# Attention and two expert layers on one core: an order from latest times, values in column tiles, and unsplit scores for the first 8 pairs

## The chip, the cores and the metric

The kernel runs on one core of a Trainium2 chip. The metric is device time in microseconds, median of three runs; less is better. Engines in the tables: PE is TensorE (matmuls; PEld its weight loads), DVE is VectorE, ACT is ScalarE, POOL is GpSimd, SP is SyncE, which issues the transfers.

## What is computed

Attention with a threshold below the row's maximum, then two feed-forward layers, all in float32. The sizes are 4 batches, 8 heads, 576 positions, head size 64, width 512, inner width 2048:

```python
scores = 0.125 * q @ k.T
thresh = max(scores) - tau
scores = where(scores >= thresh, scores, -1e9) - max(scores)
attn = exp(scores) / (sum(exp(scores)) + 1e-9)
x = (attn @ v)                  # to tokens x 512
x = softplus(x @ w1_in) @ w1_out
out = relu(x @ w2_in) ** 2 @ w2_out
```

## The kernel before

**Pairs and groups.** Attention is done in 32 pairs of two heads; a pair has one batch, half of its 576 queries (288) and two heads. Four pairs make a group of 288 tokens; there are 8 groups. A pair goes through four steps. `a_prep` (lines 269 to 274) splits the loaded q and k into a rounded part in float32r (ACT casts, L271, L272) and a rest (a subtraction on POOL, for the first pair on DVE, L273, L274). `a_scores` computes scores in nine slices of 128 keys by 288 queries from three float32r products each (high by high, low by high, high by low): the two heads sit on partitions 0 to 63 and 64 to 127, so L290 works on two row tiles of the array; the last slice has the last 64 keys of both heads and is a product over all 128 rows (L295). ACT copies each slice out of PSUM to the buffer st (L298). `a_max` finds the maximum of each query on DVE (L305, L307, L310) with four ACT copies between (L309), and spreads it over partitions as mb, for the first four pairs with L313 and L314, later with two transfers. `a_soft` subtracts it and masks (DVE, L328, L331) and exponentiates (ACT, L332). `a_out` multiplies by the values in full-precision float32, ten products a pair (L344, L345), each with 128 stationary columns: 64 of values and 64 of ones, so that one half of a PSUM bank receives the result and the other half the denominator, in 64 equal rows. ACT copies both halves out (L346, L347), DVE makes the reciprocal from a transposing reduction (L349 to L351) and multiplies (L352).

**The layers.** Layer 1 runs on one group of 288 tokens after another: `m1_up` (L368 to L370, three float32r products for each slice), softplus (ACT, L378 to L380; DVE, L381), a split (L386, L387) and `m1_down` (L399 to L401). Layer 2 runs afterwards on 512 tokens at a time (L368 to L370 and L508 to L510). Weights arrive as 64-bit words and are converted by ACT and DVE (L241 to L244) and split by POOL (L255), some through PE (L249, L250).

**What sets the order.** Each step is recorded in a `Plan` (lines 42 to 147) with its engine, an estimated duration and a key. `emit` is a list scheduler: whichever engine is free first takes the ready step with the smallest key. The keys are written by hand: pair u's steps have keys about 2u, and block k of layer 1 (a 256-wide slice of the inner width) has key k + `LAG`, with `LAG` = 13. Each engine then executes its steps in the order found.

**Buffers that the change touches.** k_r, q_r (one each), v_t (two of 1024 columns), m and rb (two each), d.

Of the kernel before, what the change touches and what calls it, by code (L numbers as in the profile page):

```python
# [26 lines left out]
LAG = 13  # L27
SPREAD = 4
EARLY = 6
PREPDVE = 1  # L30
# [11 lines left out]
class Plan:  # L42
# [6 lines left out]
    SYNC, AFTER_PE, DRAIN, LOOK, DMA_START, DMA_END, BYTES_PER_NS = 200, 300, 130, {}, 1600, 950, 300  # L49
# [20 lines left out]
    def emit(self):  # L70

        first = len(self.done)
        n = len(self.ops)
        waits = [0] * (n - first)
        users = [[] for _ in range(n - first)]
        ready_at = [0] * (n - first)
        self.done += [None] * (n - first)
        for i in range(first, n):
            for d in self.ops[i][3]:
                if d < first:  # L80
                    ready_at[i - first] = max(ready_at[i - first], self.seen(d, self.ops[i][0]))
                else:
                    waits[i - first] += 1
                    users[d - first].append(i)
        future, ready, events = {}, {}, []
        engines = {op[0] for op in self.ops[first:]}
        for e in engines:
            future[e], ready[e] = [], []
            self.free.setdefault(e, 0)
            heapq.heappush(events, (self.free[e], e))  # L90

        def release(i):
            e, key = self.ops[i][0], self.ops[i][4]
            heapq.heappush(future[e], (ready_at[i - first], key, i))
# [5 lines left out]
        left = n - first  # L100
        while left:
# [13 lines left out]
            soon = [f for f in future[e] if f[0] <= t + self.LOOK.get(e, 0) and f[1] < LAG and (not ready[e] or f[1:] < ready[e][0])]  # L115
            if soon:
                f = min(soon, key=lambda f: f[1:])
                future[e].remove(f)
                heapq.heapify(future[e])
                t, i = f[0], f[2]  # L120
            else:
                _, i = heapq.heappop(ready[e])
# [4 lines left out]
            self.free[e] = t + ns  # L127
            end = t + ns
# [4 lines left out]
            order.append((t, len(order), fn))  # L133
            left -= 1
# [5 lines left out]
        for _, _, fn in sorted(order, key=lambda x: x[:2]):  # L140
            fn()
# [9 lines left out]
def kernel(ctx: ExitStack, tc: tile.TileContext, qT, kT, vp, tau, w1i, w1o, w2i, w2o, out):  # L151
# [45 lines left out]
    v_t = many(2, [128, 1024], "v_t")  # L197
    k_r, q_r = ap.tile([128, KW], F32, name="k_r"), ap.tile([128, HALF], F32, name="q_r")
# [3 lines left out]
    m_t, r_t, mr_t = many(2, [128, 11, 9], "m"), many(1, [32, 12, 9], "r"), many(2, [32, 2, 32], "mr")  # L202
    mb_t = many(2, [128, 2, HALF], "mb")
    rb_t, d_t = many(2, [128, HALF], "rb"), many(2, [128, 9], "d")
# [4 lines left out]
    w_t = ap.tile([128, 18], F32, name="w_t")  # L209
    m_d = [dram.tile([18, 32], F32, name=f"m_d{i}") for i in range(4)]  # L210
# [47 lines left out]
    def a_load(u, key):  # L258
        g, hp = divmod(u, HP)
        b, half = divmod(g, 2)  # L260
        P.add("SP", 600, lambda: SP.dma_start(k_r, kT[b, hp]), [], ["k_r"], key, 327680)
        P.add("SP", 600, lambda: SP.dma_start(q_r, qT[b, half, hp]), [], ["q_r"], key, 147456)

    def v_load(u, key):

        g, hp = divmod(u, HP)
        P.add("SP", 600, lambda: SP.dma_start(v_t[u % 2], vp[g // 2, hp]), [], [("v", u % 2)], key, 1 << 19)

    def a_prep(u, key):
        eng, E1, n1, n2 = ("DVE", DVE, 740, 370) if u < PREPDVE else ("POOL", POOL, 1520, 750)  # L270
        P.add("ACT", 330, lambda: ACT.copy(q_h, q_r), ["q_r"], ["q_h"], key)  # L271
        P.add("ACT", 630, lambda: ACT.copy(k_h, k_r), ["k_r"], ["k_h"], key)  # L272
        P.add(eng, n2, lambda: E1.tensor_tensor(q_l, q_r, f32(q_h), op=ALU.subtract), ["q_r", "q_h"], ["q_l"], key, lock=True)  # L273
        P.add(eng, n1, lambda: E1.tensor_tensor(k_l, k_r, f32(k_h), op=ALU.subtract), ["k_r", "k_h"], ["k_l"], key, lock=True)  # L274

    def a_scores(u, key):
# [5 lines left out]
        QK = ["k_h", "k_l", "q_h", "q_l"]  # L282
        for c in range(5):
            banks = [(y_ps[i], ("y", i)) for i in (2 * (c % 2), 2 * (c % 2) + 1)] if u < EARLY else [(a_ps[i], ("a", i)) for i in range(2)]
            cs = slice(128 * c, 128 * c + 128)
            if c < 4:
                def mms(banks=banks, cs=cs):
                    for n, (k, q) in enumerate(ops):
                        for o in range(2):
                            PE.matmul(banks[o][0][:, :HALF], k[half[o], cs], q[half[o]], start=(n == 0), stop=(n == 2))  # L290
                P.add("PE", 590 * cold, mms, QK, [b[1] for b in banks], key + 0.1 * c)
            else:
                def mms(bank=banks[0][0], cs=cs):
                    for n, (k, q) in enumerate(ops):
                        PE.matmul(bank[:, :HALF], k[:, cs], q, start=(n == 0), stop=(n == 2))  # L295
                P.add("PE", 400, mms, QK, [banks[0][1]], key + 0.1 * c)
# [3 lines left out]
    def a_max(u, key):  # L300
        i = u % 2
        st, ST = st_t[u % 3], [("st", u % 3, o) for o in range(2)]
        m, r, mr, md = m_t[i], r_t[0], mr_t[i], m_d[u % 4]
        M, R, MR, MD = ("m", i), "r", ("mr", i), ("md", u % 4)
# [29 lines left out]
    def a_out(u, key):  # L334
# [4 lines left out]
        rb, RB = rb_t[u % 2], ("rb", u % 2)  # L339
        half = [slice(0, 64), slice(64, 128)]  # L340
        for o in range(2):
            bank, BK = a_ps[o][:, :HALF], ("a", o)
            for c in range(4):
                P.add("PE", 486 * cold, lambda c=c, o=o, bank=bank: PE.matmul(bank, vt[:, 192 * c + 64 * o:192 * c + 64 * o + 128], e[:, 5 * o + c], start=(c == 0), stop=False), [E[o], V], [BK], key + o)  # L344
# [258 lines left out]
```

## Time and profile before

| | |
|---|---|
| median of three runs | 1166.75 us (1165.86 to 1168.1) |
| the profiled execution | 1168.44 us, span 1166.7 us |
| mean granted PE clock | 0.978 of full speed |
| busy: PE, DVE, ACT, POOL | 1117.3, 678.0, 685.9, 247.8 us |

The profiled execution lies 1.7 us above the median. Attention and layer 1 share the first 730 us or so, layer 2 takes the rest. A busy PE means that records of matmuls cover the time; a record is longer than its slot in the stream, so durations of PE are read below from start to start. A full-precision float32 product leaves two weight loads and two matmul records, a float32r product one of each.

### The profile page before, as it was taken

The numbers are of one execution on the slowest core, as the hardware profiler recorded it, in microseconds if no ns is written. First come the engines' busy times: TensorE is split into PE (matmuls) and PEld (weight loads), VectorE is DVE, ScalarE is ACT, GpSimd is POOL, SyncE is SP. The second block draws the span as 40 slices with busy tenths as digits, with TensorE's granted clock in tenths as the row PEclk, the third lists the DMA queues.
The fourth block names the chain that finished last, engine by engine and source line by source line (L and its number), as shares of the span: only waits on it lengthen the run. The fifth ranks groups of instructions, "written<-read, shape, count | busy, mean of one in ns | idle before, by whom it ended". The sixth has DMA issues, their size and how long they took to land.

```text
span 1166.7 us, 16963 instructions
## 1 busy us (share of the span) xinstructions
PE 1117.3 (96%) x6424; PEld 953.1 (82%) x6424; DVE 678.0 (58%) x962; ACT 685.9 (59%) x1560; POOL 247.8 (21%) x222
## 2 busy tenths in 40 slices
PE   4777899999999999999999999999999999999998
PEld 3554788898898888988988899988888888888887
DVE  5998988775765756757657645888332322322232
ACT  5888888777777677777776757865222222222222
POOL 3232532342222223222223121544000000000000
PEclk9787999999999999999999999999999999999999
DMA  5346442221221312212211104764010010000010
GB/s 181 103 137 208 163 153 71 80 68 56 84 61 56 100 46 62 94 51 71 79 56 64 49 12 159 237 188 144 27 47 1 4 51 1 1 37 1 1 37 19
DMA packets 39285, 89.10 MB, mean 76 GB/s; under 512 B 6180, under 2 KB 14884, under 8 KB 39204
## 3 DMA queue, kind: packets, MB, share of 16 engines
q1 hardware_dynamic: 39204, 88.03, 23.4%
q8 instruction: 50, 0.82, 0.3%
q14 instruction: 31, 0.25, 0.1%
HBM read 78.51 MB, written 9.50 MB: 75 GB/s over the span
## 4 chain that ended last, share of the span: by engine, by line
PE 86%; DVE 8%; ACT 2%; issue 2%; DMA 2%; POOL 0%; SPq 0%; DVEq 0%; POOLq 0%; ACTq 0%
PE h_ps L368 12%; PE h_ps L370 11%; PE h_ps L369 11%; PE a_ps L344 9%; PE y_ps L399 6%; PE y_ps L508 6%; PE y_ps L509 6%; PE y_ps L510 6%; PE y_ps L401 5%; PE y_ps L400 5%; PE a_ps L290 4%; DVE st L328 2%; PE a_ps L345 2%; DVE st L331 2%; DVE wraw L242 1%
## 5 line engine op out<-in xcount | busy, mean ns | idle before, releaser
L368 PE MATMUL h_ps<-x_h,wih 128*128 128x288 f32 x512 | 161.5, 315 | 7.3 <-DVE gt L381 5.7
L399 PE MATMUL y_ps<-g_h,woh 128*128 128x288 f32 x512 | 159.4, 311 | 0.0
L387 POOL TENSOR_TENSOR g_l<-gt,g_h 128x288 fp32r<-128x288 f32 x96 | 83.2, 872 | 340.8 <-ACT g_h L386 255.6
L370 PE MATMUL h_ps<-x_h,wil 128*128 128x288 f32 x512 | 153.2, 299 | 0.0
L369 PE MATMUL h_ps<-x_l,wih 128*128 128x288 f32 x512 | 151.4, 296 | 0.0
L401 PE MATMUL y_ps<-g_l,woh 128*128 128x288 f32 x512 | 151.1, 295 | 0.0
L344 PE MATMUL a_ps<-st,v_t 128*128 128x288 f32 x512 | 144.0, 426 | 7.4 <-ACT st L332 7.4
L400 PE MATMUL y_ps<-g_h,wol 128*128 128x288 f32 x512 | 150.9, 295 | 0.0
L488 ACT ACTIVATE r<-h_ps 128x512 f32<-128x512 f32 (+1 forms) x80 | 44.4, 555 | 151.5 <-PE h_ps L370 151.5
L489 DVE SCALAR_TENSOR_TENSOR r<-h_ps,r 128x512 f32<-128x512 f32 (+1 forms) x80 | 51.0, 638 | 135.9 <-ACT r L488 135.9
L381 DVE SCALAR_TENSOR_TENSOR gt<-h_ps,a_t 128x288 f32<-128x288 f32 x128 | 57.4, 451 | 124.2 <-ACT a_t L380 123.7
L344 PEld LDWEIGHTS a_ps<-st,v_t 128*128 128x128 f32 x512 | 99.5, 199 | 34.8 <-ACT st L332 9.1
L328 DVE TENSOR_TENSOR st<-st,mb 64x288 f32<-64x288 f32 (+1 forms) x128 | 124.5, 992 | 2.0 <-DMA mb<-m_d 0.9
L495 ACT CAST g_h<-r 128x512 fp32r<-128x512 f32 (+1 forms) x80 | 46.2, 578 | 125.9 <-PE y_ps L509 125.7
L369 PE MATMUL h_ps<-y_l,wih 128*128 128x512 f32 (+1 forms) x320 | 120.0, 375 | 0.0
L368 PE MATMUL h_ps<-y_h,wih 128*128 128x512 f32 (+1 forms) x320 | 119.2, 372 | 0.0
L370 PE MATMUL h_ps<-y_h,wil 128*128 128x512 f32 (+1 forms) x320 | 118.7, 371 | 0.0
L496 DVE TENSOR_TENSOR g_l<-r,g_h 128x512 fp32r<-128x512 f32 (+1 forms) x80 | 51.0, 637 | 110.8 <-ACT g_h L495 110.7
L509 PE MATMUL y_ps<-wol,g_h 128*128 128x512 f32 x288 | 114.1, 396 | 0.0
L508 PE MATMUL y_ps<-woh,g_h 128*128 128x512 f32 x288 | 114.1, 396 | 0.0
L510 PE MATMUL y_ps<-woh,g_l 128*128 128x512 f32 x288 | 114.0, 396 | 0.0
L368 PEld LDWEIGHTS h_ps<-x_h,wih 128*128 128x128 f32 x512 | 97.8, 191 | 18.7 <-DVE gt L381 7.8
(101 smaller groups left out, 2456.2 us busy)
## 6 DMA issues: line engine op xcount, KB each, us to landing
v_t<-in_vp SPq DMA_DIRECT2D x32, 512.0 KB
k_r<-in_kT SPq DMA_DIRECT2D x32, 320.0 KB
wraw<-in_w1i SPq DMA_DIRECT2D x16, 512.0 KB
wraw<-in_w1o SPq DMA_DIRECT2D x16, 512.0 KB
wraw<-in_w2i SPq DMA_DIRECT2D x16, 512.0 KB
wraw<-in_w2o SPq DMA_DIRECT2D x16, 512.0 KB
mb<-m_d SPq DMA_DIRECT2D x28, 288.0 KB
q_r<-in_qT SPq DMA_DIRECT2D x32, 144.0 KB
```

Source lines behind the costliest of these rows:

```text
L328: DVE.tensor_tensor(st[p0:p1, a:a + n], st[p0:p1, a:a + n], mb[p0:p1, o:o + 1].to_broadcast([p1 - p0, n, HALF]), op=ALU.subtract),
L344: P.add("PE", 486 * cold, lambda c=c, o=o, bank=bank: PE.matmul(bank, vt[:, 192 * c + 64 * o:192 * c + 64 * o + 128], e[:, 5 * o + c], sta ...
L368: PE.matmul(bank, wih[p][:, c, f], xh[c], start=(c == 0), stop=False)
L369: PE.matmul(bank, wih[p][:, c, f], xl[c], start=False, stop=False)
L370: PE.matmul(bank, wil[p][:, c, f], xh[c], start=False, stop=(c == 3))
L387: P.add(eng, ns, lambda j=j: e.tensor_tensor(g_hl[1][j], gt_t[j], f32(g_hl[0][j]), op=ALU.subtract), [("gt", j), ("g_h", j)], [("g_l", j)] ...
L399: PE.matmul(o, woh[p][:, j, es], g_h[j], start=first, stop=False)
L400: PE.matmul(o, wol[p][:, j, es], g_h[j], start=False, stop=False)
L401: PE.matmul(o, woh[p][:, j, es], g_l[j], start=False, stop=last)
L508: PE.matmul(o, g_h[j][:, ts], woh[p][:, j], start=first, stop=False)
L509: PE.matmul(o, g_h[j][:, ts], wol[p][:, j], start=False, stop=False)
L510: PE.matmul(o, g_l[j][:, ts], woh[p][:, j], start=False, stop=last)
```

## The change

1. **Order.** `emit` runs the list scheduler 24 times. After each round a backward pass works out, from the end of that round's order, how late each step could run, and these latest times are the keys of the next round; the shortest round by the plan's own estimates is used. `LAG` becomes 12 (the first round's keys), and some estimated durations change.
2. **Values in column tiles.** A pair's values are 8 products with 64 stationary columns, the two heads in the two halves of one PSUM bank, and one product of 128 columns for the last keys. The denominators are 8 products with 32 columns of ones, in four column tiles of another bank, and one of 128 columns. Each head's denominator arrives in two partial sums, so ACT copies four pieces across partitions (L441 of the changed kernel) and DVE adds them (L442). One eviction of 128 partitions takes the place of two of 64. The values' transfer shrinks from 512 to 320 KB.
3. **Scores without a split.** For the first 8 pairs (`RAW`) `a_prep` does nothing, and each slice of scores is one full-precision product of the loaded k and q in place of three float32r products. k_r and q_r have two buffers each; m and rb have one in place of two.

```diff
-LAG = 13
+LAG = 12
-PREPDVE = 1
+RAW = 8
...
+    def emit(self, rounds=24):
...
+        keys = [op[4] for op in self.ops[first:]]
+        best = None
+        for r in range(rounds):
+            self.free, self.bus, self.lock = dict(state[0]), *state[1:]
+            order = self.forward(first, users, keys)
+            length = max(self.free.values())
+            if best is None or length < best[0]:
+                best = length, order, self.done[first:], (self.free, self.bus, self.lock)
+            keys = self.backward(first, users, order)
...
     def a_prep(u, key):
...
+        if u < RAW:
+            return
...
+        if u < RAW:
+            ops, QK, last, ns = [(k_rt[u % 2], q_rt[u % 2])], [("k_r", u % 2), ("q_r", u % 2)], 0, [590, 590]
...
+        X, D = a_ps[0][:, :HALF], a_ps[1][:, :HALF]
+        AX0, AD = ("a", 0), ("a", 1)
+        for c in range(4):
+            def mms(c=c):
+                for o in range(2):
+                    PE.matmul(X[64 * o:64 * o + 64], vt[:, 256 * o + 64 * c:256 * o + 64 * c + 64], e[:, 5 * o + c], start=(c == 0), stop=False)
+            P.add("PE", (490 + 100 * (c == 0)) * cold, mms, E + [V], [AX0], key)
+        for c in range(0, 4, 2):
+            def mms(c=c):
+                for o in range(2):
+                    for i in range(2):
+                        a = 64 * o + 32 * i
+                        PE.matmul(D[a:a + 32], one_t, e[:, 5 * o + c + i], start=(c == 0), stop=False)
+            P.add("PE", (490 + 100 * (c == 0)) * cold, mms, E, [AD], key)
+        P.add("PE", 590 * cold, lambda: PE.matmul(X, vt[:, 512:], e[:, 4], start=False, stop=True), [E[0], V], [AX0], key)
+        P.add("PE", 490 * cold, lambda: PE.matmul(D, onb_t, e[:, 4], start=False, stop=True), [E[0]], [AD], key)
+        P.add("ACT", 310, lambda: ACT.copy(xf, X), [AX0], [XF], key - 0.5)
+        P.add("ACT", 310, lambda: ACT.copy(rb, D), [AD], [RB], key - 0.5)
...
+        for a in range(4):
+            b = a ^ 1
+            P.add("ACT", 220, lambda a=a, b=b: ACT.copy(d[32 * a:32 * a + 32, 1], d[32 * b:32 * b + 32, 0]), [DN], [("d2", u % 2)], key + 0.5)
+        P.add("DVE", 140, lambda: DVE.scalar_tensor_tensor(out=d[:, 0], in0=d[:, 0], scalar=1e-9, in1=d[:, 1], op0=ALU.add, op1=ALU.add), [("d2", u % 2)], [DN], key + 1)
```

**PE, one pair's products with the values in the middle of the program.** Before, the ten products of a pair stand together (a_ps are the two PSUM banks, st the exponentials, v_t the values):

```order
L295 MATMUL a_ps_145<-q_h,k_h 128x288
L295 MATMUL a_ps_145<-q_h,k_l 128x288
L295 MATMUL a_ps_145<-q_l,k_h 128x288
L344 MATMUL a_ps_146<-st_156,v_t_148 128x288 x2
L344 MATMUL a_ps_145<-st_156,v_t_148 128x288 x4
L345 MATMUL a_ps_145<-st_156,v_t_148 128x288
L344 MATMUL a_ps_146<-st_156,v_t_148 128x288 x2
L345 MATMUL a_ps_146<-st_156,v_t_148 128x288
L399 MATMUL y_ps_63<-g_h_132,woh_86 128x288
```

Now (L423 values in two column tiles, L430 denominators in four, L432 and L433 the products of 128 columns, L461 to L463 and L492 to L494 layer 1):

```order
L463 MATMUL h_ps_68<-x_h_125,wil_84 128x288
L430 MATMUL a_ps_146<-st_157,one_t 32x288 x8
L433 MATMUL a_ps_146<-st_157,onb_t 128x288
L461 MATMUL h_ps_68<-x_h_126,wih_76 128x288
...
L494 MATMUL y_ps_66<-g_l_133,woh_91 128x288
L423 MATMUL a_ps_145<-st_157,v_t_148 64x288 x8
L432 MATMUL a_ps_145<-st_157,v_t_148 128x288
L492 MATMUL y_ps_63<-g_h_132,woh_91 128x288
```

The denominators and the values now stand apart, with products of layer 1 between, so PE goes from 128 stationary columns to column tiles and back twice for this pair. Counted over PE's whole order, changes between whole-array products, row tiles and column tiles rise from 216 to 353; from the ninth pair's values on, from 176 to 273.

**DVE, the start of the program.** Before (k_l, q_l the split of the first pair, wraw and wt weights, m, mr and mb the maximum of a pair, st its scores):

```order
L274 TENSOR_TENSOR k_l<-k_r,k_h 128x640
L273 TENSOR_TENSOR q_l<-q_r,q_h 128x288
L242 TENSOR_SCALAR wraw_183<-wraw_183 128x512
L243 SCALAR_TENSOR_TENSOR wt_185<-wt_185,wraw_183 128x512
L305 TENSOR_REDUCE m_158<-st_155 128x81
...
L310 TENSOR_REDUCE mr_161<-r_160 32x18
L243 SCALAR_TENSOR_TENSOR wt_185<-wt_185,wraw_183 128x512
L314 STREAM_TRANSPOSE mb_163<-w_t 128x576
L328 TENSOR_TENSOR st_155<-st_155,mb_163 128x1152 x2
```

Now:

```order
L383 TENSOR_REDUCE m_160<-st_157 128x81
...
L388 TENSOR_REDUCE mr_162<-r_161 32x18
L383 TENSOR_REDUCE m_160<-st_158 128x81
L392 STREAM_TRANSPOSE mb_164<-w_t 128x576
L385 TENSOR_REDUCE m_160<-m_160 128x2x9
L406 TENSOR_TENSOR st_157<-st_157,mb_164 128x1152 x2
```

The split of the first pair is gone, and the second pair's large reduction (L383, st_158) stands between the first pair's small reduction and the transpose that waits for ACT's copies of it.

## Rows read from the trace of the kernel before

**Rows 1.** The page: busy time of PE, and its busy tenths in 40 slices.

```profile
PE 1117.3 (96%) x6424; PEld 953.1 (82%) x6424; DVE 678.0 (58%) x962; ACT 685.9 (59%) x1560; POOL 247.8 (21%) x222
...
PE   4777899999999999999999999999999999999998
```

**Rows 2.** Four stretches: busy time (records) of PE, PEld, DVE, ACT, POOL; clock; transfers.

```profile
0.00:204.20 204.20, 160.97 (x848) 125.84 (x849) 170.83 (x234) 159.10 (x370) 66.66 (x52) 0.87 0.44 145
204.20:691.00 486.80, 484.92 (x3255) 431.15 (x3254) 314.90 (x442) 353.89 (x864) 132.17 (x134) 1.00 0.21 65
691.00:816.70 125.70, 125.20 (x754) 113.50 (x753) 93.65 (x136) 86.12 (x178) 48.76 (x36) 1.00 0.52 169
816.70:1166.70 350.00, 346.25 (x1575) 282.60 (x1573) 98.60 (x150) 86.83 (x150) 0.24 (x1) 1.00 0.05 19
```

**Rows 3.** Timeline of PE around one slice of scores: start us, record's us, what.

```profile
323.94 0.29 PE L370 MATMUL h_ps<-x_h,wil 128*128 128x288 f32 x1
324.17 0.40 PE L290 MATMUL a_ps<-q_h,k_h 64*128 64x288 f32 x2
324.41 0.29 PE L290 MATMUL a_ps<-q_h,k_l 64*128 64x288 f32 x2
324.54 0.29 PE L290 MATMUL a_ps<-q_l,k_h 64*128 64x288 f32 x2
324.76 0.40 PE L399 MATMUL y_ps<-g_h,woh 128*128 128x288 f32 x1
325.00 0.29 PE L400 MATMUL y_ps<-g_h,wol 128*128 128x288 f32 x1
```

**Rows 4.** Timeline of PE: one pair's products with the values.

```profile
335.58 3.07 PE L344 MATMUL a_ps<-st,v_t 128*128 128x288 f32 x12
338.49 0.65 PE L345 MATMUL a_ps<-st,v_t 128*128 128x288 f32 x2
338.97 1.13 PE L344 MATMUL a_ps<-st,v_t 128*128 128x288 f32 x4
```

**Rows 5.** Groups by line, whole run: busy us, mean ns, idle before.

```profile
L344 PE MATMUL a_ps<-st,v_t 128*128 128x288 f32 x512 | 144.0, 426 | 7.4 <-ACT st L332 7.4
L345 PE MATMUL a_ps<-st,v_t 128*128 128x288 f32 x128 | 41.3, 407 | 0.0
L347 ACT ACTIVATE rb<-a_ps 64x288 f32<-64x288 f32 x64 | 25.9, 405 | 0.8
L309 ACT COPY r<-m 32x27 f32<-32x27 f32 x128 | 27.0, 211 | 3.0 <-DVE m L307 0.7
L350 DVE RECIPROCAL d<-d 128x9 f32<-128x9 f32 x32 | 6.5, 202 | 0.2
```

**Rows 6.** Waits of DVE, 0 to 204 us: total us, times, longest.

```profile
DVE mb L314 <- ACT w_t L313: 5.3, 3, 3.4
DVE d L349 <- ACT rb L347: 4.3, 3, 2.4
...
DVE k_l L274 <- ACT k_h L272: 1.7, 1, 1.7
```

**Rows 7.** Groups of POOL, 0 to 204.2 us: the split of k and q.

```profile
L274 POOL TENSOR_TENSOR k_l<-k_r,k_h 128x640 fp32r<-128x640 f32 x10 | 18.3, 1828 | 3.7 <-issue 3.3 <-ACT k_h L272 0.2 <-POOL q_l L273 0.2
L273 POOL TENSOR_TENSOR q_l<-q_r,q_h 128x288 fp32r<-128x288 f32 x10 | 8.4, 843 | 34.1 <-ACT q_h L271 34.0
```

**Rows 8.** Line 242 on DVE, 0 to 204.2 us.

```profile
L242 DVE TENSOR_SCALAR wraw<-wraw 128x512 uint32<-128x512 uint32 x32 | 19.8, 621 | 2.4 <-DMA wraw<-in_w1i 2.4
```

**Rows 9.** Line 242 in the whole run: duration in ns, least, median, greatest.

```profile
L242 DVE TENSOR_SCALAR wraw<-wraw x64: 373/422/1751, 9.6 to 810.4; 128x512 uint32<-128x512 uint32 x64
```

**Rows 10.** Groups of ACT, whole run: the casts of k and q.

```profile
L272 ACT CAST k_h<-k_r 128x640 fp32r<-128x640 f32 x32 | 23.3, 729 | 3.3 <-DMA k_r<-in_kT 3.2
L271 ACT CAST q_h<-q_r 128x288 fp32r<-128x288 f32 x32 | 13.7, 427 | 0.0
```

**Rows 11.** A wait of PE, 0 to 204 us.

```profile
PE y_ps L290 <- POOL k_l L274: 6.8, 3, 2.8
```

More of the change, by code (lines that the diff above doesn't have):

```diff
@@ L99, in emit @@
         order = []
-        left = n - first
-        while left:
+        while len(order) < n - first:
             best = None
@@ L114, in emit @@
                 heapq.heappush(ready[e], (key, i))
[L115 to L122, printed above, removed]
+            _, i = heapq.heappop(ready[e])
             eng, ns, fn, deps, key, nbytes, lock = self.ops[i]
@@ L126, in emit @@
                 self.lock = t + ns
-            self.free[e] = t + ns
-            end = t + ns
+            self.free[e] = end = t + ns
             if nbytes:
@@ L196 @@
     KW = 512 + 128
-    v_t = many(2, [128, 1024], "v_t")
-    k_r, q_r = ap.tile([128, KW], F32, name="k_r"), ap.tile([128, HALF], F32, name="q_r")
+    v_t = many(2, [128, 640], "v_t")
+    k_rt, q_rt = many(2, [128, KW], "k_r"), many(2, [128, HALF], "q_r")
     k_h, k_l = (ap.tile([128, KW], F32R, name=f"k_{n}") for n in "hl")
@@ L209 @@
     w_t = ap.tile([128, 18], F32, name="w_t")
+    one_t, onb_t = ap.tile([128, 32], F32, name="one_t"), ap.tile([128, 128], F32, name="onb_t")
+    POOL.memset(one_t, 1.0)
+    POOL.memset(onb_t, 0.0)
+    for o in range(2):
+        POOL.memset(onb_t[64 * o:64 * o + 64, 64 * o:64 * o + 32], 1.0)
     m_d = [dram.tile([18, 32], F32, name=f"m_d{i}") for i in range(4)]
@@ L289, in mms @@
                         for o in range(2):
-                            PE.matmul(banks[o][0][:, :HALF], k[half[o], cs], q[half[o]], start=(n == 0), stop=(n == 2))
-                P.add("PE", 590 * cold, mms, QK, [b[1] for b in banks], key + 0.1 * c)
+                            PE.matmul(banks[o][0][:, :HALF], k[half[o], cs], q[half[o]], start=(n == 0), stop=(n == last))
+                P.add("PE", ns[0] * cold, mms, QK, [b[1] for b in banks], key + 0.1 * c)
             else:
@@ L338, in a_out @@
         xf, XF = xf_t[u % NX], ("xf", u % NX)
[L339 to L344, printed above, removed]
-            P.add("PE", 486 * cold, lambda o=o, bank=bank: PE.matmul(bank, vt[:, 768 + 128 * o:896 + 128 * o], e[:, 4], start=False, stop=True), [E[0], V], [BK], key + o)
-            P.add("ACT", 310, lambda o=o, bank=bank: ACT.copy(xf[half[o]], bank[half[o]]), [BK], [XF], key + o - 0.5)
-            P.add("ACT", 310, lambda o=o, bank=bank: ACT.activation(rb[half[o]], bank[half[1 - o]], AF.Copy, bias=1e-9), [BK], [RB], key + o - 0.5)
@@ L348, in a_out @@
-        d, DN = d_t[u % 2], ("d", u % 2)
-        P.add("DVE", 380, lambda: DVE.tensor_reduce(d, rb.rearrange("p (b i) -> p b i", i=32), axis=AX.X, op=ALU.max, apply_transpose=True), [RB], [DN], key + 1)
-        P.add("DVE", 140, lambda: DVE.reciprocal(d, d), [], [DN], key + 1)
-        P.add("DVE", 380, lambda: DVE.transpose(rb, d.unsqueeze(2).to_broadcast([128, 9, 32])), [DN], [RB], key + 1)
+        rb, RB = rb_t[0], "rb"
+        X, D = a_ps[0][:, :HALF], a_ps[1][:, :HALF]
+        AX0, AD = ("a", 0), ("a", 1)
@@ L374, in m1_up @@
         p = k % NP
-        up([(h_ps[j][:, :HALF], ("h", j)) for j in range(2)], p, *x_hl, lambda c: [("x_h", c), ("x_l", c)], 131, key)
+        up([(h_ps[j][:, :HALF], ("h", j)) for j in range(2)], p, *x_hl, lambda c: [("x_h", c), ("x_l", c)], 133, key)
         for j in range(2):
```

136 lines of the change are left out of this document (97 added, 39 removed).

## Prediction

> **What bounds the kernel now.** I read the page first: PE is busy for 1117.3 us of a span of 1166.7, and its 40 slices are nearly full from the eighth on [rows 1]. So the question goes to stages. The table of four stretches [rows 2] shows PE busy for 161.0 of the first 204.2 us, at a granted clock of 0.87, and for 484.9 of the next 486.8 us, at 1.00; layer 2 is as full as that except for 3.8 us at its end. In the first stretch DVE has 170.8 us of work and ACT 159.1; each waits for the other and PE for both. From 204 us on both have slack and PE alone sets the pace. So there are two prices. After 204 us a microsecond of PE counts in full, and work of ACT, DVE, POOL or of transfers counts nothing; before it the reverse holds nearly.
>
> Second, the timeline of PE, for what a product costs from start to start. Twelve records of L344 and two of L345 take 335.58 to 338.97 us, 0.242 us a record [rows 4]. A full-precision product has two records (640 in all for 32 pairs of ten products [rows 5]), so 0.485 us, and a pair's ten cost 4.85 us. A float32r product takes a slot of 0.13 us, and two row tiles share one: L290's x2 rows start 0.13 us apart [rows 3]. There too is the price of a change of tiles: from L370 (323.94) to the second product after the slice (325.00) pass 1.06 us, in which five slots of 0.13 make 0.65; the remaining 0.41 us is two changes, **0.2 us each**. A change into row tiles and back is seen as 0.23 and 0.24 us between starts where 0.13 would do.
>
> **The change, part by part.** PE is bound from about the ninth pair on, so 24 of 32 pairs are charged to PE.
>
> *Products with the values.* The trace of before has no column tiles and no full-precision product in a tile. If the tiles of a set run side by side, as the two row tiles do [rows 3], the four sets of two with values, the two sets of four with denominators and the two whole products cost eight times 0.485, 3.88 us: 0.97 less a pair, 23.3 us over 24. If nothing runs side by side they are 18 products, 8.73 us: 3.88 more a pair, 93 us. I take side by side, since L290 is the nearest row: other tiles, but the same array, and there two cost as much as one.
>
> *Changes of tiles.* From the ninth pair on PE's order has 273 in place of 176. 97 more at 0.2 us are 19.4 us, with nothing beside them since PE is the bound. Bounds: 0.1 us each (column tiles load a quarter or half of the columns) to 0.25, so 10 to 24 us. **So the column tiles win almost nothing by themselves: 23.3 less 19.4, 3.9 us.**
>
> *ACT and DVE for them.* Two evictions of 128 partitions take the place of four of 64, each about 0.4 us (L347 [rows 5]), so ACT saves 0.8 us, and pays four copies of 0.211 us (L309 [rows 5]): nothing. DVE gets one addition on 9 columns, for which the reciprocal's 0.2 us (L350 [rows 5]) is the nearest row. After 204 us this is covered by slack (315 of 487 us busy [rows 2]); before, 8 pairs cost 1.6 us. The addition waits for ACT's four copies, and behind it on DVE stand reciprocal, transpose and multiplication; since rb is now single, the next pair's eviction waits for that multiplication and holds a PSUM bank that scores need. A pair comes every 20 us or so after 204 us (24 pairs in 487 us), a chain of a few microseconds, so I price this at nothing; without that distance it would be about a microsecond a pair.
>
> *Scores without a split.* Per pair PE pays five full-precision slices in place of fifteen slots: 2.42 for 1.95 us, 3.8 us for 8 pairs, in a stretch where PE is idle for 43 us [rows 2]: nothing, at most 3.8. ACT loses two casts a pair, 0.73 and 0.43 us [rows 10], 9.2 us over 8 pairs. ACT paces the start only in turn with DVE, so I take half, 4.6 (bounds 0 and 9.2). POOL loses its subtractions for all but two of the ten pairs that it splits in that stretch: 0.8 of 26.7 us [rows 7], 21.4 of 66.7 us of POOL work there [rows 2]. DVE instructions are slower at the start: L242 takes 621 ns against a median of 422 [rows 8, 9], 6.4 us over 32. If POOL's work is what slows them and they gain by its share, 0.32, that is 2.0 us (0 to 6.4). PE's wait of 6.8 us for the split of k [rows 11] ends too, but what is late next is DVE, so I don't count it again.
>
> *Order.* DVE is idle for 33.4 us of the first stretch [rows 2]. Three of its waits are of the kind that the new order or the missing split removes: 5.3 us for the copies ahead of the transpose (the second pair's large reduction now stands there), 4.3 for the denominators' eviction, 1.7 for the cast of the first k [rows 6]. I take all three, 11.3 us. Bounds: nothing, since every wait removed can return at another place, and some 25 us, if most of the idle time goes. What the order can't change is DVE's work ahead of layer 1: by the two orders the first and the sixteenth softplus results stand behind nearly the same DVE steps, with 17 against 18 and 32 against 32 weight slices.
>
> *The rest.* The smaller transfers of values and the second buffers of k_r and q_r touch transfers, with a share of 0.21 after 204 us [rows 2]: nothing. Layer 2 is not touched; its stretch stays.
>
> **The sum.** Start: 11.3 + 4.6 + 2.0 - 1.6 = 16.3 us less. PE-bound part: 3.9 less. Against the profiled execution, 1168.4 - 20.2 = 1148.2 us; it lies 1.7 us over the median, so **1146.5 us**, 1.7% faster. This case's own range: the start gives 0 to 33 us and the tiles -0.7 (changes at 0.25) to 13 (at 0.1), so 1130 to 1163.
>
> **The rivals.**
>
> *The second half holds the next tile back (slower).* The two records of a full-precision product use one tile: the second can't start before the first is through, 0.242 us later [rows 4]. If PE starts products strictly in order, the next tile's first half can start only together with that second half. Then n tile products take n + 1 steps of 0.242 us however many tiles there are: nine steps for the values, nine for the denominators, four for the two whole products, 5.33 us a pair, 0.48 more than before in place of 0.97 less. Over 24 pairs that is 11.5 us, with the changes 19.4, less the start's 16.3: 1168.4 + 14.6 - 1.7 = 1181 us, 1.3% slower. It decides from 4.72 us a pair on (4.85, less 0.81 for four changes, plus the start's 16.3 over 24). For it: the two records are there, and nothing in the trace shows a product overtaking one ahead of it. Against it: L290's pairs share slots, but float32r has one record, so they can't tell. The Trainium skill (TensorE: Matmul & The Clock Gate, Part 3, What overlaps and what doesn't) says that matmuls start and end strictly in program order and only weight loads are pulled ahead; by that rule this rival would hold for the denominators' sets of four. No row here shows it for column tiles.
>
> *The order brings nothing at the start.* The waits go elsewhere, as DVE's work ahead of layer 1 is the same. Then only the tiles' 3.9 us and perhaps a little remain: 1163 us. For it: both orders have the same DVE work before the first result of layer 1. Against it: 33.4 us of idle time that isn't forced.
>
> *The tiles don't run side by side at all.* 93 + 19.4 - 16.3: 1263 us. The row tiles speak against it.
>
> **How the numbers follow.** The forecast has 0.48, the held-back tiles 0.36, the order that brings nothing 0.13, tiles one after another 0.03. A measurement of this kernel can tell about 0.2%, 2.3 us. The forecast's range is faster but for 0.02; of the third case I put 0.09 on faster (1163 is 0.3% below) and 0.03 on no change, the rest slower; of the second 0.02 on faster and 0.02 on no change, if the start gives nearly twice what I take. Together 0.57 faster, 0.07 the same, 0.36 slower. The range leaves out 1263 us and the ends of both main cases: 1128 to 1190 us.
>
> **What would show it.** Right: in the middle of the program, a set of two tiles with values starts 0.485 us after the one before, and a set of four denominators too; the eight values and the one whole product take 2.4 us, the denominators 1.5; PE is full from about 188 us on; DVE is idle for some 20 us before that. Wrong: denominators at 0.97 us a set or evenly 0.242 us a product (the held-back tiles); PE full only from 204 us on (the order); changes of tiles far from 0.2 us; PE idle after 200 us behind an eviction of rb.

## The result and the profile after

The changed kernel takes 1135.41 us (median of four runs, 1134.42 to 1136.77) where the kernel before takes 1166.88 us beside it: **0.9731 of the time, 95% interval 0.9714 to 0.9748**, 31.5 us less. The profiled execution takes 1134.85 us with a span of 1133.1 us, 33.6 us less than that of before. The prediction was 1146.5 us, within 1128 to 1190: faster, as forecast, by half as much again.

The page after, its busy time and PE's 40 slices:

```profile
PE 1100.4 (97%) x6864; PEld 889.3 (78%) x6864; DVE 698.5 (62%) x992; ACT 675.9 (60%) x1608; POOL 260.2 (23%) x212
...
PE   6878999999999999999999999999999999999998
```

PE's slices are at 90% or more from the fifth on (113 us), where before it was the sixth (146 us) [rows 1]. Its busy time is 16.9 us less, its idle time (span less busy) falls from 49.4 to 32.7 us. The table of the first two stretches and of the third, with the columns of [rows 2]:

```profile
0.00:204.20 204.20, 176.58 (x1094) 121.20 (x1094) 180.48 (x263) 164.48 (x415) 53.54 (x49) 0.94 0.46 146
204.20:691.00 486.80, 486.68 (x3712) 406.86 (x3711) 338.94 (x476) 361.68 (x921) 162.11 (x133) 1.00 0.20 61
691.00:816.70 125.70, 124.48 (x635) 105.63 (x634) 90.97 (x118) 71.94 (x137) 44.57 (x30) 1.00 0.47 143
```

In the first 204.2 us PE works 15.6 us more than before and DVE 9.7 us more [rows 2]. From there on PE is as full as it was, and nothing waits for the eviction that rb, now single, could have held up. Layer 1's softplus results on DVE (L474, L381 before; 128 in all) mark where the time comes from. The first starts at 97.8 us (before 115.7), the 17th at 184.1 (207.0), the 33rd at 264.9 (295.2), the last at 722.0 (754.8). From the last one to the end of the span it is 411.1 us (411.9). So 30.3 of 32.8 us stand before 300 us, 17.9 of them before the first result, and layer 2 gives 0.8.

The timeline of PE after, around two places with column tiles, one with denominators and values together, one with denominators alone:

```profile
313.01 0.29 PE L373 MATMUL a_ps<-q_l,k_h 128*128 128x288 f32 x1
313.24 1.18 PE L430 MATMUL a_ps<-st,one_t 128*32 128x288 f32 x16
314.34 2.16 PE L423 MATMUL a_ps<-st,v_t 128*64 128x288 f32 x16
316.44 0.75 PE L432 MATMUL a_ps<-st,v_t 128*128 128x288 f32 x2
...
332.85 0.29 PE L463 MATMUL h_ps<-x_h,wil 128*128 128x288 f32 x1
333.07 1.18 PE L430 MATMUL a_ps<-st,one_t 128*32 128x288 f32 x16
334.18 0.75 PE L433 MATMUL a_ps<-st,onb_t 128*128 128x288 f32 x2
334.55 0.51 PE L461 MATMUL h_ps<-x_h,wih 128*128 128x288 f32 x1
334.90 0.29 PE L462 MATMUL h_ps<-x_l,wih 128*128 128x288 f32 x1
```

Seen in narrow windows, the records of L430 come in fours (these two lines stop at 313.45 and at 313.55 us):

```profile
313.24 0.45 PE L430 MATMUL a_ps<-st,one_t 128*32 128x288 f32 x4
313.24 0.69 PE L430 MATMUL a_ps<-st,one_t 128*32 128x288 f32 x8
```

Eight denominators (16 records of L430) take 1.10 us from start to start, eight products with values (L423) 2.10, each with one change of tiles in it (from 32 to 64 columns counts as one). Two sets of four at 0.485 us are 0.97, four sets of two 1.94: **the tiles of a set run side by side**, though each product has two records. One excursion can be priced from the second place: after L463's slot of 0.13 us, at 332.98, to L461's start as its successor sets it (334.90 less 0.13, 334.77) pass 1.79 us; three sets of 0.485 are 1.455, so two changes cost 0.33 us, **0.17 us each**.

Groups by line after, beside [rows 5], and the wait of the transpose that stood first in [rows 6] (DVE, 0 to 204 us):

```profile
L441 ACT COPY d<-d 32x9 f32<-32x9 f32 x128 | 25.2, 196 | 4.7 <-DVE d L438 2.3
L435 ACT COPY rb<-a_ps 128x288 f32<-128x288 f32 x32 | 12.8, 401 | 6.8 <-PE a_ps L433 5.0 <-DVE st L409 0.8 <-DVE xf L445 0.4
L442 DVE SCALAR_TENSOR_TENSOR d<-d 128x9 f32<-128x9 f32 x32 | 10.2, 320 | 9.6 <-ACT d L441 9.3
...
DVE d L438 <- ACT rb L435: 3.6, 4, 1.2
...
DVE mb L392 <- ACT w_t L391: 0.4, 1, 0.4
```

The copies and evictions cost what they were taken for, the addition (L442) 320 ns where 200 were taken. The wait for the first transposes is nearly gone, 0.4 us in place of 5.3; that for the denominators' eviction is nearly what it was, 3.6 for 4.3 [rows 6].

### The profile page after: what moved, and what is told of

It is laid out like the page before. It is cut to its first block, busy times and chain, and to the rows that moved or that the text cites. A ratio compares the mean times of both kernels' runs of the same rounds, so it can differ in the third digit from the quotient of the medians.

```text
span 1133.1 us, 17947 instructions
## 1 busy us (share of the span) xinstructions
PE 1100.4 (97%) x6864; PEld 889.3 (78%) x6864; DVE 698.5 (62%) x992; ACT 675.9 (60%) x1608; POOL 260.2 (23%) x212
## 4 chain that ended last, share of the span: by engine, by line
PE 85%; DVE 8%; ACT 3%; issue 2%; DMA 1%; SPq 0%; DVEq 0%; ACTq 0%
PE h_ps L461 12%; PE h_ps L462 11%; PE h_ps L463 11%; PE y_ps L492 6%; PE y_ps L602 6%; PE y_ps L601 6%; PE y_ps L603 6%; PE a_ps L368 5%; PE y_ps L494 5%; PE y_ps L493 5%; PE a_ps L423 5%; PE a_ps L430 3%; DVE st L406 1%; DVE m L383 1%; PE a_ps L433 1%
## 5 line engine op out<-in xcount | busy, mean ns | idle before, releaser
L461 PE MATMUL h_ps<-x_h,wih 128*128 128x288 f32 x512 | 161.8, 316 | 1.9 <-DVE gt L474 1.6
L480 POOL TENSOR_TENSOR g_l<-gt,g_h 128x288 fp32r<-128x288 f32 x96 | 111.5, 1166 | 226.1 <-ACT g_h L479 214.3
L492 PE MATMUL y_ps<-g_h,woh 128*128 128x288 f32 x512 | 161.7, 316 | 0.0
L494 PE MATMUL y_ps<-g_l,woh 128*128 128x288 f32 x512 | 151.2, 295 | 0.4 <-DVE g_l L480 0.4
L463 PE MATMUL h_ps<-x_h,wil 128*128 128x288 f32 x512 | 151.3, 295 | 0.0
L406 DVE TENSOR_TENSOR st<-st,mb 64x288 f32<-64x288 f32 (+1 forms) x128 | 131.3, 1045 | 9.1 <-DMA mb<-m_d 8.1
L588 ACT CAST g_h<-r 128x512 fp32r<-128x512 f32 (+1 forms) x80 | 46.2, 578 | 124.5 <-PE y_ps L602 124.5
L463 PE MATMUL h_ps<-y_h,wil 128*128 128x512 f32 (+1 forms) x320 | 118.8, 371 | 0.6 <-POOL wil L328 0.6
L461 PE MATMUL h_ps<-y_h,wih 128*128 128x512 f32 (+1 forms) x320 | 119.2, 373 | 0.0
L474 DVE SCALAR_TENSOR_TENSOR gt<-h_ps,a_t 128x288 f32<-128x288 f32 x128 | 57.6, 451 | 84.2 <-ACT a_t L473 82.7
L461 PEld LDWEIGHTS h_ps<-x_h,wih 128*128 128x128 f32 x512 | 96.2, 188 | 16.8 <-issue 11.6
L409 DVE SCALAR_TENSOR_TENSOR st<-st,thr 128x1152 f32<-128x1152 f32 (+1 forms) x64 | 104.8, 1641 | 0.3
L492 PEld LDWEIGHTS y_ps<-g_h,woh 128*128 128x128 f32 x512 | 96.5, 188 | 10.2 <-issue 8.2
```

What stands on the lines that cost most here:

```text
L406: DVE.tensor_tensor(st[p0:p1, a:a + n], st[p0:p1, a:a + n], mb[p0:p1, o:o + 1].to_broadcast([p1 - p0, n, HALF]), op=ALU.subtract),
L409: P.add("DVE", 315 * (s1 - s0), lambda x=x: DVE.scalar_tensor_tensor(out=x, in0=x, scalar=thr, in1=x, op0=ALU.is_lt, op1=ALU.subtract), [] ...
L461: PE.matmul(bank, wih[p][:, c, f], xh[c], start=(c == 0), stop=False)
L463: PE.matmul(bank, wil[p][:, c, f], xh[c], start=False, stop=(c == 3))
L480: P.add(eng, ns, lambda j=j: e.tensor_tensor(g_hl[1][j], gt_t[j], f32(g_hl[0][j]), op=ALU.subtract), [("gt", j), ("g_h", j)], [("g_l", j)] ...
L492: PE.matmul(o, woh[p][:, j, es], g_h[j], start=first, stop=False)
```

## The experiments

The change has three parts. **The theory of the order**: most of the gain is the new order's, and my term for it, 11.3 us, was too small. **The theory of the split**: it is the missing split that feeds DVE and takes POOL off its back, and the order is what I took it for. **The theory of the tiles**: they gain more than 3.9 us where PE is the bound. Each part was taken away alone and done alone.

In the table (PE busy, idle, first, last and clock are from each kernel's profiled execution) idle is the span less PE's busy time; first and last are the starts of the first and the last softplus result, in us. Each ratio is taken against runs of before on the same chip in the same series, whose medians were 1166.88 to 1169.06 us; where the text gives a gain in us, it is the ratio's distance from 1 of that median.

| kernel | order | unsplit | tiles | us | ratio to before (95%) | PE busy | idle | first | last | clock |
|---|---|---|---|---|---|---|---|---|---|---|
| before | - | - | - | 1166.88 | 1 | 1117.3 | 49.4 | 115.7 | 754.8 | 0.978 |
| order_only | x | - | - | 1143.23 | 0.9783 (0.9767-0.9800) | 1110.5 | 30.6 | 98.5 | 729.8 | 0.984 |
| raw_only2 | - | x | - | 1161.97 | 0.9942 (0.9929-0.9956) | 1116.3 | 43.7 | 109.2 | 748.2 | 0.985 |
| tiles_only | - | - | x | 1169.44 | 1.0001 (0.9992-1.0011) | 1107.8 | 60.1 | 124.5 | 756.1 | 0.969 |
| no_order | - | x | x | 1161.22 | 0.9944 (0.9929-0.9959) | 1107.9 | 51.5 | 109.0 | 747.4 | 0.980 |
| no_raw | x | - | x | 1150.18 | 0.9841 (0.9826-0.9855) | 1104.4 | 42.8 | 109.2 | 736.2 | 0.979 |
| no_tiles2 | x | x | - | 1137.36 | 0.9731 (0.9718-0.9745) | 1107.3 | 28.6 | 96.6 | 724.7 | 0.993 |
| after | x | x | x | 1135.41 | 0.9731 (0.9714-0.9748) | 1100.4 | 32.7 | 97.8 | 722.0 | 0.989 |

The last column is the mean granted clock of PE, which moves between two levels, 2.4 GHz (1.00) and 1.2 GHz. By it before spends about 2 x (1 - 0.978) x 1166.7 = 51 us at the lower level, order_only 37, the changed kernel 25, tiles_only 72, nearly all of it at the start, where PE also waits most. At the lower level a float32r product takes a slot of 0.24 us (before, from 180.86 to 183.02 us) where it takes 0.13 at the upper [rows 3]. In order_only PE is busy for 6.8 us less than before with the same 6424 records, so a part of what the order brings comes with the clock. No run holds the clock fixed; how much of a gain is the clock's stays open.

**The order taken away** (no_order), the changed kernel with one round, so that the order comes from the hand-written keys:

```diff
-    def emit(self, rounds=24):
+    def emit(self, rounds=1):
```

> The changed kernel with the first round of the scheduler alone (hand-written keys, LAG 12). The changed kernel takes 1135 us. Split theory (most of the 26 us gained ahead of the PE-bound part come from the scores without a split, the order adds little): 1135 to 1142 us, since the order gives about 6 us and its fewer changes of tiles here (238 against 273 from the ninth pair on, 0.165 us each) give 6 back. Order theory (the new order fills the waits and gives most of them): 1150 us or more.

Measured 1161.22 us, 0.9944: of the gain of 2.69% remain 0.56. The theory of the order holds.

**The unsplit scores taken away** (no_raw):

```diff
-RAW = 8
+RAW = 0
```

> The changed kernel with all 32 pairs split (RAW 0). Split theory: 1150 us or more, POOL busy for some 20 us more before 146 us and DVE's instructions slow again (mask subtraction of 1152 columns near 1600 ns, as before, in place of 1346). Order theory: 1141 us, DVE's idle time as low as in the changed kernel.

Measured 1150.18 us, 0.9841: 1.1 of the 2.69% go. That is the figure of the theory of the split (1150 us or more), not the 1141 us of the theory of the order, and the large mask subtraction is slow again (1635 ns over the first 146 us). But it is more than the split is worth by itself (below): against order_only (0.9783) the tiles, here without the unsplit scores, cost 0.6%. In no_raw POOL and not DVE splits the first pair, whose large maximum starts at 14.01 us in place of 12.26, so not all of that need be the tiles'.

**The tiles taken away** (no_tiles, no_tiles2), the changed kernel with `a_out`, the values' layout and their transfer of before:

```diff
+                P.add("PE", 486 * cold, lambda c=c, o=o, bank=bank: PE.matmul(bank, vt[:, 192 * c + 64 * o:192 * c + 64 * o + 128], e[:, 5 * o + c], start=(c == 0), stop=False), [E[o], V], [BK], key + o)
```

> The changed kernel with the ten whole-array products per pair of before (second buffers of the first loads lie in buffers of layer 1 that are not yet in use). Both theories: the products and the changes of tiles in the changed kernel's trace (0.485 us a set, 0.165 us a change, 97 more changes) make 4.85 - 4.55 = 0.30 us a pair over 24 pairs, so 7 us more: 1142 us. If the tiles also help or hurt ahead of the PE-bound part: outside 1138 to 1146.

Measured 1139.40 us, 0.9750 (0.9735 to 0.9764), about 2 us more than the changed kernel and not 7. To make room for the larger v_t, the second buffers of k_r and q_r lay here in buffers of layer 1, for the pairs 1, 3 and 5 only, and the loads of pairs 7 and 8 came ahead of the scores of pairs 6 and 7: these two pairs multiplied the next pair's q and k, in the same amount of work. So it was done again with those two loads behind the scores:

```diff
-                    if u + 1 < NU:
+                    if u + 1 < NU and u not in (6, 7):
                         a_load(u + 1, s - 1)
                     a_scores(u, s)
+                    if u in (6, 7):
+                        a_load(u + 1, s - 1)
```

> The changed kernel with the ten whole-array products of before, as in no_tiles, but with the loads of pairs 7 and 8 recorded behind the scores of pairs 6 and 7, so that these two pairs get their own q and k. Theory (the tiles are worth 2.2 us at the end, and the wrong operands of two pairs did not move the time): 0.974 to 0.976. Rival (the loads that came too early shortened no_tiles): slower than that, 0.978 or more.

Measured 1137.36 us, 0.9731: the same as the changed kernel, below even the 0.974 that was expected. **With the order and the unsplit scores there, the tiles bring nothing that can be measured.**

**The order alone** (order_only), the kernel before with the new `Plan`, `LAG` 12 and the new estimates of durations:

```diff
-LAG = 13
+LAG = 12
...
+    def emit(self, rounds=24):
...
+            keys = self.backward(first, users, order)
```

> The kernel before with the new order alone (24 rounds, LAG 12, the changed estimates), split and whole-array products as before. Split theory: 1160 us. Order theory: 1148 us or less.

Measured 1143.23 us, 0.9783: **25.4 us of the 31.5 are the order's alone.** DVE's groups up to the first softplus result show how, first in the kernel before (0 to 115.7 us), then here (0 to 98.5 us):

```profile
L328 DVE TENSOR_TENSOR st<-st,mb 128x1152 f32<-128x1152 f32 (+1 forms) x21 | 23.1, 1131 | 1.2 <-DMA mb<-m_d 0.9
L305 DVE TRANSPOSE_TENSOR_REDUCE m<-st 128x81 f32<-128x2592 f32 x7 | 20.1, 2864 | 1.5 <-ACT st L298 1.5
L243 DVE SCALAR_TENSOR_TENSOR wt<-wt,wraw 128x512 uint32<-128x512 uint32 x17 | 13.0, 772 | 1.9 <-ACT wt L241 1.8
L314 DVE STREAM_TRANSPOSE mb<-w_t 128x576 f32<-128x576 f32 x4 | 3.1, 765 | 5.3 <-ACT w_t L313 5.3
L349 DVE TRANSPOSE_TENSOR_REDUCE d<-rb 128x9 f32<-128x288 f32 x5 | 2.4, 478 | 1.7 <-ACT rb L347 1.5
```

```profile
L395 DVE TENSOR_TENSOR st<-st,mb 128x1152 f32<-128x1152 f32 (+1 forms) x20 | 19.6, 981 | 1.4 <-DMA mb<-m_d 1.2
L372 DVE TRANSPOSE_TENSOR_REDUCE m<-st 128x81 f32<-128x2592 f32 x6 | 17.2, 2864 | 2.7 <-ACT st L365 2.7
L310 DVE SCALAR_TENSOR_TENSOR wt<-wt,wraw 128x512 uint32<-128x512 uint32 x16 | 11.7, 734 | 0.9 <-ACT wt L308 0.6
L381 DVE STREAM_TRANSPOSE mb<-w_t 128x576 f32<-128x576 f32 x4 | 3.1, 769 | 1.9 <-ACT w_t L380 1.9
L416 DVE TRANSPOSE_TENSOR_REDUCE d<-rb 128x9 f32<-128x288 f32 x4 | 1.9, 472 | 0.0
```

A pair's large maximum, the fifth pair's denominator and a weight slice no longer stand ahead of the first result, though four pairs are all that it needs; and DVE waits less. The table of stretches counts it together:

```profile
0.00:115.70 115.70, 79.95 (x335) 53.72 (x336) 94.93 (x122) 87.33 (x206) 33.29 (x31) 0.82 0.48 156
```

```profile
0.00:98.50 98.50, 75.17 (x312) 49.67 (x312) 85.83 (x112) 80.60 (x192) 29.79 (x29) 0.83 0.52 168
```

Of the 17.2 us by which the first result is earlier, 9.1 are less DVE work ahead of it (94.93 to 85.83) and 8.1 less idle time (20.8 to 12.7). Ten instructions fewer stand ahead of the result (122 to 112); at the mean times of before they make 7.6 us, and the other 1.5 are instructions that take less time here. The rest comes between the first and the 33rd result, which starts at 270.6 us, 24.6 earlier; from there on the distance stays within 3 us (last 25.0). Over the first 204.2 us:

```profile
0.00:204.20 204.20, 177.85 (x997) 140.77 (x998) 181.61 (x252) 169.94 (x409) 72.52 (x58) 0.92 0.48 155
```

DVE is idle there for 22.6 us in place of 33.4 [rows 2], 10.8 less, and the granted clock is 0.92 in place of 0.87.

**The new planner without its backward pass** (keys_one), order_only with one round:

```diff
-    def emit(self, rounds=24):
+    def emit(self, rounds=1):
```

> The kernel before with the new planner, its estimates and LAG 12, but with one round: the order then comes from the hand-written keys alone. Theory (the latest times of the backward pass are what shortens the start, and not the new estimates or LAG): the gain of the order alone, 25.4 us, is gone; 0.995 to 1.005 of before, first softplus result after 110 us. Rival (the new estimates or LAG 12 do it): about 0.98, first softplus result before 103 us.

Measured 1176.75 us, 1.0071 (1.0056 to 1.0086); first result at 108.1, last at 763.8, PE idle for 56.1 us. That is slower than the 0.995 to 1.005 expected, but the gain is gone. The estimates, `LAG` and the new forward pass, which were not taken apart, together cost 0.7%. So the repeated rounds with latest times are worth 2.9% over their own first round.

**The tiles alone** (tiles_only), `a_out` and the values' layout of the changed kernel in the kernel before:

```diff
+                    PE.matmul(X[64 * o:64 * o + 64], vt[:, 256 * o + 64 * c:256 * o + 64 * c + 64], e[:, 5 * o + c], start=(c == 0), stop=False)
...
+                        PE.matmul(D[a:a + 32], one_t, e[:, 5 * o + c + i], start=(c == 0), stop=False)
```

> The kernel before with the column tiles alone (its own order from hand-written keys). By the prices in the changed kernel's trace: 24 x 0.97 = 23.3 us less for products, 89 more changes of tiles at 0.165 = 14.7 us more, so 8.6 us less than 1167: 1158 us, by either theory.

Measured 1169.44 us, 1.0001: nothing, in place of 8.6 us. The page and the first 150 us of it, and of the kernel before, show that nothing is a difference of two terms:

```profile
PE 1107.8 (95%) x6936; PEld 899.6 (77%) x6936; DVE 697.3 (60%) x994; ACT 683.0 (58%) x1624; POOL 251.6 (22%) x226
...
0.00:150.00 150.00, 100.36 (x526) 57.54 (x527) 122.93 (x156) 106.48 (x256) 52.95 (x44) 0.76 0.45 145
```

```profile
0.00:150.00 150.00, 109.32 (x506) 79.97 (x506) 127.52 (x163) 115.07 (x262) 50.05 (x40) 0.84 0.48 157
```

PE's busy time falls by 9.5 us, as the tiles promise, and its idle time grows by 10.7 (49.4 to 60.1), nearly all of it, 9.0, in the first 150 us: DVE and ACT too do less in these 150 us, and the first result is 8.8 us later. Up to that result DVE has 98.9 us of work in place of 94.9 and 25.6 us of idle time in place of 20.8, and PE's granted clock over the 150 us is 0.76 in place of 0.84. In the new order it is the same: against order_only, no_raw has 6.1 us less of PE's work and 12.2 us more idle time, against no_tiles2 the changed kernel 6.9 less and 4.1 more. What makes the start longer (both heads' exponentials are now needed before the first set of values, ACT's four copies and DVE's addition stand in the chain, rb is single in no_raw, the clock) was not taken apart.

**The unsplit scores alone** (raw_only, raw_only2), with the second buffers of k_r and q_r in the same way as in no_tiles:

```diff
-PREPDVE = 1
+RAW = 8
...
+        if u < RAW:
+            return
```

> The kernel before with the unsplit scores of the first 8 pairs alone (hand-written keys, whole-array products; second load buffers in buffers of layer 1 not yet in use). Split theory: 1150 us or less. Order theory: 1160 us.

Measured 1164.18 us, 0.9960 (0.9944 to 0.9975), pairs 6 and 7 again with the next pair's operands. With the two loads behind the scores:

> The kernel before with unsplit scores for the first 8 pairs, as in raw_only, with the same correction for pairs 6 and 7. Theory: 0.995 to 0.997 as in raw_only, the missing split brings 4 to 5 us by itself. Rival (the early loads helped): 0.999 to 1.001.

Measured 1161.97 us, 0.9942: 6.8 us by themselves, a little more than in the first form. The order's 25.4 and these 6.8 make 32.2; both together, no_tiles2, give 0.9731, 31.4 us. They add up. Where the 6.8 come from shows up to the first result, at 109.2 us in raw_only2. Its row of the table of stretches, then the first weight step in before (0 to 115.7 us), and both here:

```profile
0.00:109.20 109.20, 79.97 (x270) 46.95 (x270) 87.68 (x120) 79.61 (x192) 15.22 (x18) 0.89 0.51 161
```

```profile
L242 DVE TENSOR_SCALAR wraw<-wraw 128x512 uint32<-128x512 uint32 x17 | 10.2, 607 | 2.4 <-DMA wraw<-in_w1i 2.4
```

```profile
L243 DVE SCALAR_TENSOR_TENSOR wt<-wt,wraw 128x512 uint32<-128x512 uint32 x18 | 12.2, 678 | 3.2 <-ACT wt L241 3.1
L242 DVE TENSOR_SCALAR wraw<-wraw 128x512 uint32<-128x512 uint32 x18 | 7.2, 400 | 7.6 <-DMA wraw<-in_w1i 6.9 <-DMA wraw<-in_w1o 0.6
```

DVE is idle for 21.5 us ahead of that result, not less than the 20.8 of before; it works 7.2 us less (94.93 to 87.68). By the mean times of each shape about 5.4 of these are instructions that take less time, the two weight steps above all (before L243 took 772 ns); POOL works 15.2 us there in place of 33.3.

**POOL's subtractions put back** (raw_pool), as work of the same size on buffers that nothing else uses then; the result is not touched:

```diff
+        if 0 < u < RAW:
+            P.add("POOL", 750, lambda: POOL.tensor_tensor(q_l, q_r, q_r, op=ALU.subtract), [QR], ["q_l"], key)
+            P.add("POOL", 1520, lambda: POOL.tensor_tensor(k_l, k_r, k_r, op=ALU.subtract), [KR], ["k_l"], key)
```

> The changed kernel in which POOL does again a subtraction on each loaded q and k of pairs 1 to 7 (the loaded data from itself, into the unused rest buffers); nothing reads them, ACT's casts stay out. If POOL's work slows DVE (11.6 us of DVE time in the first 146 us by the two traces): 1143 us or more, with the mask subtraction of 1152 columns back near 1600 ns. If the gain is from ACT's casts or the shorter chain ahead of the scores: 1136 us.

Measured 1141.21 us, 0.9756 (0.9725 to 0.9787), between the two figures and not told apart from the change; but the interval is wide (1136.47 to 1143.72 us), and it doesn't exclude that POOL's work costs all of the 6.8 us. In the profiled execution the first softplus result starts at 104.9 us in place of 97.8. DVE up to it, first in the changed kernel, then here, each shape by itself:

```profile
0.00:97.80 97.80, 73.30 (x340) 37.01 (x340) 83.87 (x117) 75.99 (x192) 13.53 (x21) 0.88 0.54 171
...
L406 DVE TENSOR_TENSOR st<-st,mb 128x1152 f32<-128x1152 f32 x10 | 13.3, 1350 | 0.0
L316 DVE SCALAR_TENSOR_TENSOR wt<-wt,wraw 128x512 uint32<-128x512 uint32 x18 | 12.2, 679 | 1.2 <-ACT wt L314 1.0
L315 DVE TENSOR_SCALAR wraw<-wraw 128x512 uint32<-128x512 uint32 x18 | 7.3, 408 | 3.0 <-DMA wraw<-in_w1i 2.9
```

```profile
0.00:104.90 104.90, 77.34 (x352) 37.02 (x352) 90.81 (x119) 78.95 (x197) 33.90 (x37) 0.89 0.51 163
...
L409 DVE TENSOR_TENSOR st<-st,mb 128x1152 f32<-128x1152 f32 x10 | 13.7, 1390 | 0.0
L316 DVE SCALAR_TENSOR_TENSOR wt<-wt,wraw 128x512 uint32<-128x512 uint32 x18 | 14.9, 825 | 3.0 <-ACT wt L314 2.8
L315 DVE TENSOR_SCALAR wraw<-wraw 128x512 uint32<-128x512 uint32 x19 | 8.8, 463 | 3.0 <-DMA wraw<-in_w1i 2.6 <-DMA wraw<-in_w1o 0.3
```

DVE's work ahead of the first result is nearly the same list (119 instructions for 117) and takes 6.9 us more; that is nearly all of the 7.1 us by which the result is later. So with POOL busy again for 33.9 us in place of 13.5 DVE's instructions are longer, as they are in before against raw_only2. It points to POOL and does not show it: each is one profiled execution, the order is planned anew in each kernel, and in no_tiles2, which has none of these subtractions, the two weight steps take 463 and 821 ns in the first 97.8 us. The large mask subtraction goes by something else: it takes 1578 ns in before, 1560 in raw_only2 without POOL's subtractions (first 97.8 us), and 1390 here with them. Why stays open.

**ACT's casts put back** (raw_act), in the same way:

```diff
+            P.add("ACT", 330, lambda: ACT.copy(q_h, q_r), [QR], ["q_h"], key)
+            P.add("ACT", 630, lambda: ACT.copy(k_h, k_r), [KR], ["k_h"], key)
```

> The changed kernel in which ACT casts each loaded q and k of pairs 0 to 7 again; nothing reads the casts, POOL's subtractions stay out. If ACT's time counts at the start: 1140 us or more (9.2 us of casts, half or more of it seen). If only POOL's slowing of DVE or the shorter chain counts: 1136 us.

Measured 1138.95 us, 0.9742 (0.9727 to 0.9756): not told apart from the change either, and the first result starts at 97.7 us, where it was (97.8). By the two intervals the casts cost some 4 us at most, so they do not explain the 6.8 us by themselves; POOL's subtractions may. A third candidate was not tried apart: the second pair's large maximum stands earlier on DVE. It starts at 30.33 us before and at 18.23 us in raw_only2 (both from hand-written keys), at 22.07 in order_only and at 17.36 in the changed kernel; with POOL's or ACT's work put back it stays early, 18.82 and 17.98 us. The row of DVE's timeline before, and after:

```profile
30.33 2.88 DVE L305 TRANSPOSE_TENSOR_REDUCE m<-st 128x81 f32<-128x2592 f32 x1
```

```profile
17.36 2.88 DVE L383 TRANSPOSE_TENSOR_REDUCE m<-st 128x81 f32<-128x2592 f32 x1
```

**Fewer changes of tiles** (together), a version to beat both: a pair's 18 products with the values are one step of PE.

```diff
-            P.add("PE", (490 + 100 * (c == 0)) * cold, mms, E + [V], [AX0], key)
...
+        P.add("PE", 4400 * cold, mms, E + [V], [AX0, AD], key)
```

> The changed kernel with a pair's denominators and values as one step of PE, so that PE goes into column tiles and back once a pair, not twice. Changes of tiles from the ninth pair on: 248 in place of 273. Theory (PE is the bound there and a change costs 0.165 us): 25 changes, 4.1 us less, 1131.3 us, 0.9695 of before. Rival 1 (a longer step of PE makes the layer's products and the scores wait, and the order loses at the start what the changes give): 0.972 to 0.975, no gain over the change. Rival 2 (the longer step costs more than the changes): over 0.976.

Measured 1138.30 us, 0.9740 (0.9727 to 0.9753): no gain over the change, the first rival. PE's busy time falls by another 2.6 us (1097.8) and its idle time grows by 6.0 (38.7); the first result comes at 110.0 us, 12.2 later. What is saved where PE is the bound is lost at the start once more. None of the kernels beats the changed one.

## Why the prediction was right in its sign and too small

- **The bound and the two prices: right.** PE is full after the start, earlier than the 188 us that I named, and layer 2 stays as it is; 32.8 of the 33.6 us between the two profiled executions stand before the last softplus result. (PE's slices were 90% full from the sixth on before, not from the eighth [rows 1], so its stretch began earlier than I took it; and my 1130 to 1163 us hold the tiles at 3.9 us: with their own bounds it would have been about 1121 to 1167.) In tiles_only, no_raw and together one can read both prices: busy time and idle time of PE trade against each other.
- **Order, 11.3 us: the step that failed; it measured 25.4.** I added up three waits of DVE and took it that "what the order can't change is DVE's work ahead of layer 1", by counting weight slices. The waits were sized well: in order_only DVE is idle for 10.8 us less in the first 204.2. The count of slices was right too, but maxima, masks and denominators of later pairs stand there as well: ten instructions, 7.6 us, went behind the first result. The granted clock, which the sum does not have, is higher as well (0.92 for 0.87 over the first 204.2 us), and its share is not known. The upper bound that I gave, some 25 us, was the value. That the order does it is shown by order_only, and that it comes from the backward pass by keys_one. The rival in which the order brings nothing falls with it, as it rested on the same step.
- **Unsplit scores, 4.6 + 2.0 us: right in size, but not by these two terms.** They measured 6.8 alone. ACT's casts, the 4.6, put back leave the first result where it is and cost some 4 us at most. POOL's effect on DVE, the 2.0, looks larger than I took it: DVE's instructions up to the first result are about 5.4 us shorter without the subtractions (raw_only2) and 6.9 us longer with them put back (raw_pool). That is one execution each, so it is not shown. (POOL loses seven of its ten subtractions of each kind there, not eight, since the first pair's are DVE's: 1.8 us by my own rule.) I had set aside PE's wait for the split of k [rows 11]; DVE's idle time ahead of the first result stays what it was (21.5 for 20.8 us), so nothing speaks for counting it.
- **Products with values, 23.3 us, and changes of tiles, 19.4: the mechanism right.** Sets run side by side; a change costs 0.17 us here, not 0.2. Equal groups of four pairs in the middle of the program are 84.5 us apart in order_only (softplus results 65 and 81: 439.6 and 524.1) and 83.6 in the changed kernel (435.7 and 519.3), 0.22 us a pair, 5.4 us over 24, where I had 3.9. It is an estimate from one group: from the 33rd result to the last the two kernels take 459.2 and 457.1 us, 2.1 apart, as the groups on either side of it differ.
- **The tiles at the start, 1.6 us: too small.** I priced only DVE's addition and set the chain behind it at nothing. The idle time at the start grew by 4.1 us with the other two parts there and by 10.7 alone. Their net, 2.3 us in the sum, measured nothing: close, but luck, by two terms that were both larger.
- **The held-back tiles (1181 us): false.** By it eight denominators would take nine steps of 0.242 us, 2.18; they take 1.10, a change included. The Trainium skill (TensorE: Matmul & The Clock Gate, Part 3, What overlaps and what doesn't) has matmuls start and end strictly in program order. This trace does not speak against that: the records of L430 start in fours, 0.02 us from the first to the fourth, end in the same order, and the next four start 0.27 us after the first. What fails is my step from there to the rival, that the two records of a product follow each other before the next product's; the trace doesn't say which half a record is.
- **Tiles one after another (1263 us): false** by the same rows.

## What to carry to other kernels

Price a new order by the work that it can put behind the first result of the bound stage, all steps on the pacing engine counted, and not only by the waits that it removes. Compare two starts up to each kernel's own first result, and count work, idle time and granted clock apart: raw_pool's DVE has the same work time as the changed kernel's in the first 97.8 us (83.7 and 83.9), and 6.9 us more up to its first result. A saving on the bound engine is worth nothing until the ramp has been read too: three kernels here took 3 to 10 us off PE and returned it as idle time at the start. Take each part of a change away and do each part alone: here the sum of two parts is the whole, and the third looks like a gain in the rows of the middle and is none that can be measured.

## What was not expected of the hardware

Full-precision products, which leave two records each, run side by side in column tiles just as products of one record do in row tiles: 16 records in 1.10 us in four tiles, 0.07 us a record where whole-array products take 0.242. A change between tilings costs 0.17 us, also where the new tile has only 32 columns (two changes in 0.33 us around L430).
